# An attention, soft-MoE and feed-forward kernel: where the last back end, one expert, one copy and two steps of the background stand

## The chip, the cores and the metric

The kernel runs on one core of a Trainium2 chip. The metric is device time in microseconds (us), the median of several executions. A profiled execution gives the trace that is read here. The engines are PE (TensorE: matmuls and transposes), DVE (VectorE), ACT (ScalarE), POOL (GpSimd) and SP (SyncE, which here issues nearly all DMAs). Each runs its own instructions in order and waits on semaphores of the others.

## What is computed

Three steps, each feeding the next; B = 4, H = 8, S = 768, D = 64, 3072 tokens of 512 values, all in fp32:

```python
scores = scale * q @ k.T + bias, masked to 8 global and 96 local keys
x = softmax(scores) @ v                      # 3072 x 512

logits = x @ phi                             # 32 slots, 4 for each of 8 experts
d = softmax(logits, over tokens);  slot_input = d.T @ x
slot_out[e] = relu(slot_input[e] @ w1[e]) @ w2[e]
y = softmax(logits, over slots) @ slot_out   # 3072 x 512, of rank 32

h = y @ w_in                                 # 512 -> 2048
out = (relu(h) ** 2) @ w_out                 # 2048 -> 512
```

The feed-forward input y is a product of a 3072 x 32 matrix of weights (here c_tok, spread out as cst) with slot_out, so the kernel never forms y: for each part of w_in it computes U = slot_out @ w_in (32 rows) and then h from U.

## The kernel before

**Attention.** 48 units are worked in pairs; a unit is a pair of heads of a chunk of 256 tokens, and four units make a chunk. A unit goes through stage_qk (scores), stage_max, stage_exp, stage_T (transposes), stage_ev (copies out of PSUM, pT), stage_pv (value products, o) and stage_x (ACT copies o into the chunk's tile xT). The order on every engine is the order in which the program is written; there is no scheduler.

**Routing.** For each chunk of 256 tokens the generator `route(k)` makes the logits (into c_tok) and adds the chunk to the running softmax over tokens. Its front end makes the logits and the scaled rows xb; its back end, done for two chunks at a time, makes transposed logits pq, their maximum rmax, nm, the exponent dT (ACT, with the correction factor fo), the transposes pd of it, their copy db, the denominators rden, the product pS and its addition to acc. The generator stops at each `yield`; `step(n)` resumes the one at the head of a queue n times, `next(last)` resumes the last chunk's own (`tail`), so attention and routing are woven together by hand. In the tail the logits are made in two halves: `products(pl, range(2))` needs the first two units of the chunk, `products(pl, range(2, 4))` all four; `scaled` and `added` (DVE: lh, l, c_tok) weight and sum them, `turn` (PE: px) transposes xT. From the last chunk's pq the chain goes on through rmax, nm, dT, pd, db, pS, acc and pv to slotZ, the slots' input.

**Experts.** `w1_of(e)` multiplies slotZ by w1 of one expert on PE. The first EARLY experts come ahead of a branch (`tc.If`, into a general path that these inputs don't take), the others behind it. The weights lie in slots of SBUF: w2_0 to w2_2 are loaded when attention's tiles are given up, w2_3, w2_4, w2_5, w2_6, win_0 and wout_0 (the first parts of w_in and w_out) and w2_7 (in four pieces) each when an expert's w1 has been used. All are issued by SP in that order. `w2_of(e)` then adds up pSO; the first part of w_in and w_out, whose words are 64-bit, is converted beside it (`convert`: L750 on ACT, L751, L752 and L755 on DVE; a w_out chunk ends with a cast `hi` on ACT and a subtraction `lo`). SO is pSO copied out by ACT, pst and soT its transpose.

**Feed-forward.** Five parts of w_in and w_out, of 256, 384, 512, 512 and 384 columns, each over 12 blocks of 256 tokens. `make_u` computes pu (four matmuls with soT on the part's winf), copies it out as a high and a low half (evu), adds up four row groups in a second matmul (pu2) and writes U as a high part (ACT) in all rows, with the low part in the second and the fourth group of 32 rows (DVE, L820, one subtraction for each group). `gemm1` makes h of a block, ACT and DVE its relu and square (rg), POOL the low half of that (g); `gemm2` makes acc for half a block, three matmuls to 128 columns of the part, and DVE (or ACT) adds it to oacc. Three accumulators take turns. `make_u` for the next part and the conversion of its weights are a generator (`background`), resumed some times ahead of each half block; `total` and `room` set the pace. Between w2 and the first block PE runs filler matmuls (`warm`, tile idle).

## Time and profile before

| | us |
|---|---|
| median of 3 executions | 551.76 |
| lowest, highest | 549.9, 551.92 |
| profiled execution, its own time | 549.59 |
| its span, first to last instruction | 547.6 |
| PE busy in the span | 526.8 (96%) |
| DVE busy | 398.1 (73%) |
| ACT busy | 310.7 (57%) |
| POOL busy | 164.2 (30%) |

Attention takes the time until about 190 us, its tail and the first w1 matmul until 201, the experts until 238, the hand-over to the feed-forward until 244; the five parts then begin at about 245, 286, 345, 418 and 491 us. The share of PE is that of a busy engine, not of one at its peak. A row of a timeline gives the start, the duration, the engine, the line, the operation, what it writes and reads, the shape and a count; in brackets stands how long the engine had been idle before it and which operation released it. PEld is PE's weight load.

### The profile page before, as it was taken

Reading aid. Unit: us, or ns where it says so; the run is one execution under the profiler, and the core shown is the slowest. Engines: PE = TensorE matmul, PEld = TensorE weight load, DVE = VectorE, ACT = ScalarE, POOL = GpSimd, SP = SyncE. Lnnn points to the kernel's source line nnn. Section 1 sums busy time; section 2 is a strip of 40 time slices with the busy share of each in tenths; the row PEclk is TensorE's granted clock in tenths of the full one; section 3 lists DMA queues with packets and bytes.
Section 4 is the critical chain, followed back from the end, with each engine's and each line's share of the span. In section 5 each row is a group of like instructions: output and inputs, shape, how many; then the busy total and the mean of one; then the engine's idle time right before and its main releaser. Section 6 shows DMA issues by size and latency. Waiting matters only on the chain.

```text
span 547.6 us, 10220 instructions
## 1 busy us (share of the span) xinstructions
PE 526.8 (96%) x3669; PEld 396.9 (72%) x3669; DVE 398.1 (73%) x999; ACT 310.7 (57%) x815; POOL 164.2 (30%) x146
## 2 busy tenths in 40 slices
PE   6999999999999899989999999999999999999997
PEld 4677677777777744346878678878888878888885
DVE  4988979888888773549769797888856866645553
ACT  2888777778787611246676465545544545434441
POOL 0000000000000001014565367454754436534441
PEclk9899999999999999999999999999999999999999
DMA  7579998898972589962240404030020000003333
GB/s 258 194 252 314 314 322 304 313 338 304 317 248 85 203 312 426 414 279 58 97 154 1 154 0 156 0 116 0 21 96 1 0 2 0 1 0 116 116 116 115
DMA packets 25831, 89.20 MB, mean 163 GB/s; under 512 B 3120, under 2 KB 3760, under 8 KB 23600
## 3 DMA queue, kind: packets, MB, share of 16 engines
q1 hardware_dynamic: 25344, 88.37, 44.5%
q8 instruction: 30, 0.49, 0.4%
q14 instruction: 25, 0.20, 0.1%
q10 hardware_dynamic: 432, 0.13, 0.1%
HBM read 82.20 MB, written 6.29 MB: 162 GB/s over the span
## 4 chain that ended last, share of the span: by engine, by line
PE 44%; DVE 12%; DMA 3%; ACT 2%; issue 1%; POOL 0%; DVEq 0%; ACTq 0%; POOLq 0%
PE acc L860 13%; PE acc L861 13%; PE acc L862 13%; PE h L842 3%; DMA raw<-in_w_in 3%; DVE rg L847 2%; DVE cvyo L752 2%; DVE cvyi L752 1%; DVE cvyi L751 1%; DVE oacc L868 1%; ACT rg L846 1%; DVE cvyo L755 1%; DVE cvyo L751 1%; PE pu L801 1%; DVE winf L755 1%
## 5 line engine op out<-in xcount | busy, mean ns | idle before, releaser
L850 POOL TENSOR_TENSOR g<-rg,g 128x512 fp32r<-128x512 f32 (+1 forms) x109 | 136.2, 1251 | 174.5 <-DVE rg L847 169.2
L860 PE MATMUL acc<-w,g 128*128 128x512 f32 x384 | 151.6, 395 | 1.1 <-ACT g L849 0.6
L861 PE MATMUL acc<-w,g 128*128 128x512 f32 x384 | 150.7, 392 | 0.0
L862 PE MATMUL acc<-w,g 128*128 128x512 f32 x384 | 150.1, 391 | 0.6 <-POOL g L850 0.5
L846 ACT ACTIVATE rg<-h 128x512 f32<-128x512 f32 (+1 forms) x109 | 59.7, 547 | 118.6 <-PE h L842 114.2
L868 DVE TENSOR_TENSOR oacc<-acc,oacc 128x512 f32<-128x512 f32 x95 | 65.3, 688 | 60.8 <-PE acc L862 60.6
L255 ACT ACTIVATE sm<-sm,nm 128x256 f32<-128x256 f32 (+1 forms) x192 | 92.7, 486 | 14.3 <-DVE nm L242 11.6
L862 PEld LDWEIGHTS acc<-w,g 128*128 128x128 f32 x384 | 72.1, 188 | 18.3 <-POOL g L850 2.7
L860 PEld LDWEIGHTS acc<-w,g 128*128 128x128 f32 x384 | 72.1, 188 | 18.0 <-issue 3.2
L861 PEld LDWEIGHTS acc<-w,g 128*128 128x128 f32 x384 | 72.4, 188 | 11.2
L847 DVE SCALAR_TENSOR_TENSOR rg<-h,rg 128x512 f32<-128x512 f32 (+1 forms) x109 | 67.8, 622 | 17.2 <-ACT rg L846 17.2
L236 DVE CUSTOM_DVE_ANT_0 sm<-s,mask 128x256 f32<-128x256 f32 (+1 forms) x192 | 67.3, 396 | 1.5 <-PE s L222 1.2
L849 ACT ACTIVATE g<-rg 128x512 fp32r<-128x512 f32 (+1 forms) x109 | 63.3, 581 | 3.5
L222 PE MATMUL s<-raw 64*128 64x256 f32 (+1 forms) x384 | 52.9, 394 | 3.8 <-DVE mx L236 2.4
L388 POOL COPY l<-c_tok 128x256 f32<-128x256 f32 x11 | 4.4, 400 | 167.8 <-DVE c_tok L341 139.4
L266 PE MATMUL pt<-con,sm 128*128 128x128 f32 x352 | 47.3, 280 | 1.8 <-DVE xb L334 1.7
L283 PEld LDWEIGHTS o<-pT,v 128*64 128x64 f32 x704 | 38.0, 137 | 10.3 <-ACT pT L272 5.2
L266 PEld LDWEIGHTS pt<-con,sm 128*128 128x128 f32 x352 | 38.7, 142 | 8.9 <-DVE xb L334 3.3
L283 PE MATMUL o<-pT,v 128*64 128x128 f32 x704 | 44.3, 277 | 0.5 <-issue 0.2
L222 PEld LDWEIGHTS s<-raw 64*128 64x128 f32 x384 | 31.6, 191 | 16.2 <-issue 7.6
L842 PEld LDWEIGHTS h<-cu 128*128 128x128 f32 x192 | 35.8, 188 | 7.6 <-issue 0.3
L842 PE MATMUL h<-cu 128*128 128x256 f32 x192 | 39.8, 280 | 0.0
(150 smaller groups left out, 564.8 us busy)
## 6 DMA issues: line engine op xcount, KB each, us to landing
raw<-in_qk SPq DMA_DIRECT2D x48, 384.0 KB, 5.1
w<-in_w SPq DMA_DIRECT2D x36, 512.0 KB, 6.5
w<-in_w SPq DMA_DIRECT2D x7, 2048.0 KB, 9.5
v<-in_vx SPq DMA_DIRECT2D x48, 256.0 KB, 4.0
out_x<-oacc SPq DMA_DIRECT2D x23, 256.0 KB, 2.0
win<-in_w_in SPq DMA_DIRECT2D x2, 2048.0 KB, 7.9
wout<-in_w_out SPq DMA_DIRECT2D x2, 2048.0 KB, 8.4
win<-in_w_in SPq DMA_DIRECT2D x2, 1536.0 KB, 9.9
```

The costliest lines, as they stand in the source:

```text
L222: nc.tensor.matmul(sc[hh][:, tt, 0:n, :], lhsT=r[r0 : r0 + D, tt, :], rhs=rhs, start=True, stop=True)
L236: V.tensor_tensor_reduce(out=sm[:, j, 0:n, :], in0=sc[hh][:, tt, 0:n, :], in1=m[:, 2:3, :] if n == 1 else m[:, 0:2, :], scale=1.0, scalar= ...
L255: nc.scalar.activation(sm[:, j, 0:n, :], sm[:, j, 0:n, :], AF.Exp, bias=nm[:, j : j + 1], scale=QK_SCALE, accum_out=chunk_sums(i // NPR)[: ...
L266: nc.tensor.transpose(pp[tt][:, hh, c, :], sm[:, 2 * tt + hh, c, :], ident)
L283: nc.tensor.matmul(o[hh * D : hh * D + D, tt, :], lhsT=v[:, tt + 2 * c, hh * D : hh * D + D], rhs=pT[:, 2 * tt + hh, c, :], start=c == 0, ...
L842: nc.tensor.matmul(ph[:, k, :], lhsT=U[:, c0 : c0 + P], rhs=cst[:, n * TB : n * TB + TB], start=True, stop=True)
L847: V.scalar_tensor_tensor(g, ph[:, k0:k1, :], 0.0, r, op0=ALU.max, op1=ALU.mult)
L850: G.tensor_tensor(g2[:, 1, js, :], g, g2[:, 0, js, :].bitcast(F32), op=ALU.subtract)
L860: nc.tensor.matmul(pa, lhsT=ghi[:, j, ms], rhs=whi[:, j, :], start=j == 0, stop=False)
L861: nc.tensor.matmul(pa, lhsT=ghi[:, j, ms], rhs=wlo[:, j, :], start=False, stop=False)
L862: nc.tensor.matmul(pa, lhsT=glo[:, j, ms], rhs=whi[:, j, :], start=False, stop=j == J - 1)
L868: V.tensor_tensor(o, pa, o, op=ALU.add)
```

## The change

Four edits, the last with a change of pace:

- The back end of the last pair of chunks (9 and 10) is resumed in more and smaller pieces between the steps of the last chunk. The last chunk's generator gets one more `yield` behind the second half of its products; its first products stand directly behind the last stage_pv, ahead of pd; db and rden of the pair stand behind the first half of the logits on DVE; pS stands behind px on PE.
- EARLY is 6: the sixth expert's w1 stands ahead of the branch, and with it the issue of w2_6's load.
- The last w_out chunk of the first part is converted up to its second `yield` as before, but its cast and subtraction come behind SO and soT.
- The low part of U is one operation over all 128 rows: `U * odd + pu2`, where odd is -1 in the two groups and 0 elsewhere, a column written by three memsets on POOL.
- `background` has three `yield`s in place of one between the conversion of w_in and make_u, and `total` is larger by two.

```diff
             products(pl, range(2, 4))
+            yield
             scaled(l5[:, :, 1:5, :], 4, 8)
@@ tail of attention
     stage_pv(i)
     stage_x(i)
-    step(1)
     stage_pv(i + 1)
-    step(2)
     last = route(NU // NPR - 1, True)
     next(last)
     step(1)
     stage_x(i + 1)
+    step(2)
     next(last)
     step(1)
     next(last)
-    step(1000)
+    next(last)
+    step(2)
     queue.append(last)
@@ experts
-    EARLY = 5
+    EARLY = 6
@@ behind the branch
+    odd = ex.tile([P, 1], F32, tag="odd", name="odd")
+    G.memset(odd, 0.0)
+    for r0 in (NS, 3 * NS):
+        G.memset(odd[r0 : r0 + NS], -1.0)
@@ make_u
         nc.scalar.copy(U, pu2[:, 0:W])
-        for r0 in (NS, 3 * NS):
-            V.tensor_tensor(U[r0 : r0 + NS, :], pu2[r0 : r0 + NS, 0:W], U[r0 : r0 + NS, :].bitcast(F32), op=ALU.subtract)
+        V.scalar_tensor_tensor(U, U.bitcast(F32), odd, pu2[:, 0:W], op0=ALU.mult, op1=ALU.add)
@@ w2 of expert 6
-            for c in conv_out(0):
-                for _ in c:
-                    pass
+            c0, c1 = conv_out(0)
+            for _ in c0:
+                pass
+            next(c1)
+            next(c1)
@@ behind soT
+    for _ in c1:
+        pass
@@ background
-        for _ in range(1):
+        for _ in range(3):
             yield
@@ pace
-            total, room = 5 * (WIDTHS[q + 1] // P) + 5, 2 * (NBLK - AHEAD) - 1
+            total, room = 5 * (WIDTHS[q + 1] // P) + 7, 2 * (NBLK - AHEAD) - 1
```

PE in the tail of attention, before; o is the value product, pl and pl_2 are the two halves of the last logits:

```order
L283 MATMUL o_2932<-pT_2902,v_2776 64x128 x8
L434 MATMUL pd_2941<-con,dT_2927 128x32 x4
L326 MATMUL pl_2948<-phib,xT_2852 128x64 x4
L326 MATMUL pl_2_2965<-phib,xT_2852 128x64 x4
L452 MATMUL pS_2972<-xb_2632,db_2955 32x512 x2
L452 MATMUL pS_2972<-xb_2802,db_2955 32x512 x2
L331 MATMUL px_0_2949<-con,xT_2852 128x128 x4
```

The same place after:

```order
L283 MATMUL o_2923<-pT_2902,v_2776 64x128 x8
L326 MATMUL pl_2934<-phib,xT_2852 128x64 x4
L435 MATMUL pd_2951<-con,dT_2945 128x32 x4
L326 MATMUL pl_2_2962<-phib,xT_2852 128x64 x4
L331 MATMUL px_0_2935<-con,xT_2852 128x128 x4
L453 MATMUL pS_2976<-xb_2632,db_2967 32x512 x2
L453 MATMUL pS_2976<-xb_2802,db_2967 32x512 x2
```

The first half of the logits has moved ahead of pd, and px ahead of pS. DVE at the same place, before:

```order
L439 COPY db_2955<-pd_2941 128x128
L440 SCALAR_TENSOR_TENSOR rden<-rden,fo_2925,dn_2926 128x1
L366 TENSOR_SCALAR rc_2946<-sums_2700 128x16
L367 RECIPROCAL rc_2946<-rc_2946 128x16
L338 TENSOR_TENSOR lh_2961<-pl_2948,rc_2946 128x2x128
L341 TENSOR_REDUCE l_2962<-lh_2961 128x2x32
L338 TENSOR_TENSOR l_2962<-pl_2_2965,rc_2946 128x2x128
```

And after:

```order
L366 TENSOR_SCALAR rc_2932<-sums_2700 128x16
L367 RECIPROCAL rc_2932<-rc_2932 128x16
L338 TENSOR_TENSOR lh_2958<-pl_2934,rc_2932 128x2x128
L341 TENSOR_REDUCE l_2959<-lh_2958 128x2x32
L440 COPY db_2967<-pd_2951 128x128
L441 SCALAR_TENSOR_TENSOR rden<-rden,fo_2943,dn_2944 128x1
L338 TENSOR_TENSOR l_2959<-pl_2_2962,rc_2932 128x2x128
```

db and rden have moved from the front to between the two halves. ACT between w2 and the feed-forward, before:

```order
L790 CAST w_10268<-cvyo_10270 128x512
L750 ACTIVATE cvxo_10277<-raw_10117 128x512
L790 CAST w_10268<-cvyo_10278 128x512
L904 COPY SO<-pSO 128x512
L808 COPY evu_10324<-pu_10319 128x256
```

And after:

```order
L795 CAST w_10281<-cvyo_10283 128x512
L755 ACTIVATE cvxo_10290<-raw_10130 128x512
L911 COPY SO<-pSO 128x512
L795 CAST w_10281<-cvyo_10291 128x512
L813 COPY evu_10337<-pu_10332 128x256
```

SO and the second cast have changed places. DVE in the second part, while the third part's w_in is converted, from the third chunk's last operation on, before:

```order
L755 SCALAR_TENSOR_TENSOR winf_10746<-cvxi_10815,cvyi_10816 128x512
L868 TENSOR_TENSOR oacc_10349<-acc_2_0_10839,oacc_10349 128x512
L847 SCALAR_TENSOR_TENSOR rg_4_0_10853<-h_4_0_10850,rg_4_0_10853 128x512
L751 TENSOR_SCALAR cvyi_10859<-win_10742 128x512
L752 SCALAR_TENSOR_TENSOR cvyi_10859<-win_10742,cvyi_10859 128x512
L868 TENSOR_TENSOR oacc_10349<-acc_2_1_10863,oacc_10349 128x512
L847 SCALAR_TENSOR_TENSOR rg_4_1_10876<-h_4_1_10874,rg_4_1_10876 128x256
L755 SCALAR_TENSOR_TENSOR winf_10746<-cvxi_10858,cvyi_10859 128x512
L868 TENSOR_TENSOR oacc_10349<-acc_3_0_10882,oacc_10349 128x512
L847 SCALAR_TENSOR_TENSOR rg_5_0_10896<-h_5_0_10893,rg_5_0_10896 128x512
L805 TENSOR_TENSOR evu_10906<-pu_10901,evu_10906 128x512
L868 TENSOR_TENSOR oacc_10349<-acc_3_1_10909,oacc_10349 128x512
```

And after:

```order
L760 SCALAR_TENSOR_TENSOR winf_10757<-cvxi_10826,cvyi_10827 128x512
L756 TENSOR_SCALAR cvyi_10851<-win_10753 128x512
L757 SCALAR_TENSOR_TENSOR cvyi_10851<-win_10753,cvyi_10851 128x512
L873 TENSOR_TENSOR oacc_10361<-acc_2_0_10855,oacc_10361 128x512
L852 SCALAR_TENSOR_TENSOR rg_4_0_10869<-h_4_0_10866,rg_4_0_10869 128x512
L760 SCALAR_TENSOR_TENSOR winf_10757<-cvxi_10850,cvyi_10851 128x512
L873 TENSOR_TENSOR oacc_10361<-acc_2_1_10875,oacc_10361 128x512
L852 SCALAR_TENSOR_TENSOR rg_4_1_10888<-h_4_1_10886,rg_4_1_10888 128x256
L873 TENSOR_TENSOR oacc_10361<-acc_3_0_10893,oacc_10361 128x512
L852 SCALAR_TENSOR_TENSOR rg_5_0_10907<-h_5_0_10904,rg_5_0_10907 128x512
L873 TENSOR_TENSOR oacc_10361<-acc_3_1_10912,oacc_10361 128x512
L852 SCALAR_TENSOR_TENSOR rg_5_1_10925<-h_5_1_10923,rg_5_1_10925 128x256
```

The last winf has moved ahead of the addition of acc_2_1, and evu behind that of acc_3_1. On PE, pu stands behind acc_3_1 instead of ahead of it, in all four parts that have one; pu2 keeps its place in the second and third part and moves by one half block in the first and fourth.

## Rows read from the trace of the kernel before

**Rows 1.** Stretches: us; PE, PEld, DVE, ACT, POOL busy; PEclk, DMA share, GB/s.

```profile
11.00:18.00 7.00, 5.39 (x28) 3.76 (x30) 6.83 (x35) 4.75 (x20) 1.51 (x5) 0.51 0.67 237
18.00:176.00 158.00, 154.56 (x1644) 114.28 (x1640) 133.33 (x545) 127.30 (x459) 3.60 (x9) 1.00 0.81 280
...
201.00:205.00 4.00, 4.00 (x44) 1.27 (x40) 2.89 (x6) 0.84 (x1) 0.00 (x0) 1.00 0.52 137
205.00:236.00 31.00, 30.04 (x256) 10.87 (x246) 14.90 (x28) 7.14 (x14) 1.83 (x1) 1.00 1.01 422
```

**Rows 2.** Timeline: SP's issue of w2_3, and PE at the last quarter of w2_7.

```profile
202.50 0.33 SPq L203 DMA_DIRECT2D w<-in_w  x1
...
235.99 1.05 PE L741 MATMUL pSO<-w,hZ 128*32 128x512 f32 x4 [0.22 <-DMA w<-in_w]
```

**Rows 3.** Timeline of the tail of attention, all engines.

```profile
189.81 0.69 ACT L424 ACTIVATE dT<-pq,nm 128x512 f32<-128x512 f32 x1 [0.41 <-DVE nm L423]
...
190.64 0.43 PE L434 MATMUL pd<-con,dT 32*128 32x32 f32 x4 [0.78 <-ACT dT L424]
190.68 0.36 ACT L293 COPY xT<-o 128x256 f32<-128x256 f32 x1
...
191.00 2.00 PE L326 MATMUL pl<-phib,xT 128*128 128x64 f32 x16
191.11 0.29 DVE L439 COPY db<-pd 128x128 f32<-128x128 f32 x1 [1.33 <-PE pd L434]
...
192.14 0.42 DVE L338 TENSOR_TENSOR lh<-pl,rc 128x256 f32<-128x256 f32 x1 [0.24 <-PE pl L326]
...
193.19 0.41 DVE L338 TENSOR_TENSOR l<-pl,rc 128x256 f32<-128x256 f32 x1
...
194.27 0.74 DVE L469 SCALAR_TENSOR_TENSOR acc<-acc,fo,pS 128x512 f32<-128x512 f32 x1
...
194.51 0.65 PE L406 MATMUL pq<-con,c_tok 128*32 128x128 f32 x16
...
195.22 0.42 DVE L422 TENSOR_REDUCE rmax<-pq 128x1 f32<-128x256 f32 x1 [0.21 <-PE pq L406]
```

**Rows 4.** Timeline of the hand-over from w2 to the feed-forward.

```profile
237.20 0.62 ACT L790 CAST w<-cvyo 128x512 fp32r<-128x512 f32 x1 [2.03 <-DVE cvyo L755]
237.73 0.58 ACT L904 COPY SO<-pSO 128x512 f32<-128x512 f32 x1
...
238.36 1.08 PE L909 MATMUL pst<-con,SO 128*128 128x32 f32 x8 [0.45 <-ACT SO L904]
...
241.54 1.58 PE L79 MATMUL idle<-con 128*128 128x256 bf16 x13
...
242.14 0.86 DVE L820 TENSOR_TENSOR cu<-pu,cu 32x256 fp32r<-32x256 f32 x2 [2.37 <-ACT cu L818]
```

**Rows 5.** PE's timeline at pu in the first, second and third part.

```profile
256.95 0.84 PE L801 MATMUL pu<-winf,soT 128*32 128x384 f32 x4
...
259.15 0.50 PE L860 MATMUL acc<-w,g 128*128 128x512 f32 x1
...
302.00 1.06 PE L801 MATMUL pu<-winf,soT 128*32 128x512 f32 x6
...
304.80 0.50 PE L860 MATMUL acc<-w,g 128*128 128x512 f32 x1
...
306.97 0.28 PE L842 MATMUL h<-cu 128*128 128x256 f32 x1
...
365.74 1.06 PE L801 MATMUL pu<-winf,soT 128*32 128x512 f32 x8
```

**Rows 6.** PE's timeline late in the second part.

```profile
326.28 0.47 PE L860 MATMUL acc<-w,g 128*128 128x512 f32 x1 [0.63 <-ACT g L849]
```

**Rows 7.** DVE's groups by shape: count, busy us, mean ns, idle before them.

```profile
L752 DVE SCALAR_TENSOR_TENSOR cvyi<-win,cvyi 128x512 int32<-128x512 int32 x14 | 18.3, 1308 | 0.5
...
L752 DVE SCALAR_TENSOR_TENSOR cvyi<-raw,cvyi 128x512 int32<-128x512 int32 x2 | 1.4, 692 | 0.1
```

## Prediction

> **What bounds the kernel now.** Read the stretches first [rows 1]: the columns to look at are PEclk, the DMA share and GB/s. TensorE's granted clock is at the upper level, 2.4 GHz (1.00), in every stretch from 18 us on, of which three stand there, and at 0.51 in one before. The DMA engines are full, share 1.01 at 422 GB/s, from 205 to 236 us, and half empty (137 GB/s) in the 4 us ahead of it. So the end of the w2 stage is a matter of when that transfer train sets off, and of nothing that PE does in between. Its first car is the load of w2_3, which SP issues at 202.50, when the matmuls of the first expert's w1 have freed the slot; its last is the last quarter of w2_7, for which PE waits at 235.99 [rows 2]. What comes ahead of 202.50, the tail of attention, therefore moves the start of the feed-forward part one for one, as long as the DMA engines still have an idle stretch to give up.
>
> Then the tail, in order of time [rows 3]. The exponent dT of the last chunk pair ends at 190.50. PE has finished its value products by 189.86 (the row of pd says 0.78 us idle before 190.64, ended by dT) and stands still, though the first half of the last chunk's logit products needs nothing but xT, which is there. Those 2.00 us of pl start at 191.00 behind pd; VectorE does lh at 192.14, l at 193.19; behind l comes c_tok, and pq follows at 194.51. The chain runs on from pq to slotZ and w1.
>
> Then the hand-over [rows 4]. The last pSO matmuls end at 235.99 + 1.05 = 237.04, but ScalarE copies SO at 237.73, behind a cast that ran from 237.20. Then come pst at 238.36 and the chain to U, whose two subtractions take 0.86 together.
>
> Then the feed-forward parts. From PE's own rows [rows 5] the four matmuls of pu (the next part's U) take 1.06 us when all of winf is there (365.74). In the first part they and their wait fill 256.95 to 259.15, 2.20 us, in the second 302.00 to 304.80, 2.80 us: PE stands in its queue for VectorE's last conversion, with gemm2 matmuls behind that could run. One late wait more is the row at 326.28 [rows 6]. From 345 us on PE has no such row.
>
> **The change, part by part.** Every size is made against the profiled execution, 549.59 us with a span of 547.58.
>
> *Spread back end.* The first half of pl (2.00 / 2 = 1.00 us) goes into PE's idle stretch from 189.86 and ends near 190.85; pd follows at about its old time, since dT ends at 190.50 anyway; the second half can start near 191.1, when xT's last copy ends at 190.68 + 0.36. VectorE's lh was ready 1.14 us after pl's start (192.14 less 191.00) and so comes near 191.0, 1.15 earlier. From lh to l is 1.05 as before. But db (0.29) and the short rden now stand between them, where lh's wait used to hide them: some 0.3 lost, an estimate from the row of db. So l, c_tok and pq come 0.85 to 0.95 earlier. Behind c_tok, acc (0.74) used to fit into the wait for pq (194.27 to 195.01, rmax at 195.22); pS now starts behind px and ends about when acc wants it, so it still just fits. I take 0.9; the ends are 0.3 (pS late, acc pushes rmax) and 1.2 (nothing lost to db). The step is carried by the train: slotZ, w1_0, the issue at 202.50 and the last landing move together. The idle DMA stretch before it is 4 us, so it can give up 0.9.
>
> *Six experts ahead of the branch.* The same matmuls, and the same branch, one expert later. On SP the load of w2_6 moves ahead of the branch, and the loads of win_0, wout_0 and w2_7 queue behind the branch instead. With a full train [rows 1] an issue that comes a few us earlier or later changes no landing. On GpSimd three small memsets follow the branch, long before U reads them. I cost it at nothing. If the train had run dry the branch would show; an issue would have to slip by many us for that.
>
> *SO ahead of the cast.* SO starts when pSO ends, near 237.1 in place of 237.73: 0.6 off the path; ends 0.3 and 0.65. The cast (0.62) and the subtraction behind it move behind SO and soT, into time in which ScalarE and VectorE wait for PE; their result is first read by gemm2, behind U and gemm1.
>
> *U in one operation.* Two operations over 32 partitions take 0.86; one over 128 partitions with the same 256 elements has no row of before, but time goes by elements, so 0.42 to 0.47. The gain of about 0.4 meets PE's 13 filler matmuls, which run from 241.54 for 1.58 us until 243.12 whatever U does. PE gets at most the queue's slack back: I take 0.15, ends 0 and 0.43. In the later parts it takes 0.5 to 0.7 from VectorE, in the next step's account.
>
> *Two more steps ahead of make_u.* pu moves behind one more half block of gemm2. In the first part VectorE's conversions keep their order; pu without a wait costs 0.8 at three quarters of the columns of the row at 365.74, and I allow 0.3 for the half block, which may have to wait for its accumulator: 2.20 - 0.8 - 0.3 = 1.1, ends 0.3 and 1.4. In the second part the quicker pace also puts the last winf ahead of two VectorE operations, and pu wants it a half block later (304.80 to 306.97, 2.17 us): 2.80 less 1.06 = 1.74, I take 1.7, ends 0.8 and 1.75. The gap from pu to pu2 shrinks to one such half block there; a cast and a subtraction lie between, some 1.4 us by the cast at 237.20 (0.62) and acc (0.74). The conversions of w_out start one step later and are still done before the next part. In the fourth and third part nothing waits now, nothing to gain.
>
> *Late waits.* The PE wait at 326.28 (0.63 us), and about as much again spread over both parts, come from VectorE working behind. The change moves conversions behind accumulator additions there and takes a U operation out: I take 0.8, ends -0.5 (conversions now late) and 2.0.
>
> **Sum:** 0.9 + 0.6 + 0.15 + 1.1 + 1.7 + 0.8 = 5.25 us. On the profiled execution that is 549.59 to 544.3; on the median of the runs shown, 551.76, it is 546.5. Two of the three runs lie 2.2 us above the profiled one, one 0.3 above; the forecast is for the median, and this spread is in the range.
>
> **A rule weighed.** VectorE's L752 (two SBUF inputs) took 692 ns in the tail, where GpSimd is silent, and 1308 ns on average in the parts, where GpSimd subtracts [rows 7]. The Trainium skill (SBUF — State Buffer, Who interferes with whom) says that VectorE and GpSimd share a port pair as an exclusive lock, and that an operation with two SBUF inputs is blocked for the whole of a GpSimd operation that reads SBUF. By that rule the trace agrees, and moved conversions land behind other GpSimd subtractions: if each of the moved ones were blocked, the feed-forward gain would mostly go, and the sum would be that of the first rival; by the rows alone it stays at 5.25.
>
> **Rivals.** (1) *VectorE stays the bound.* The two steps only move the wait: conversions stretched from 0.69 to 1.31 or more arrive as late as PE's new place for pu, or accumulators are freed late. For it: the row of L752, and the accumulator wait that I already count in the first part. Against it: pu's new place is up to 2.17 us later. Then only the tail and the hand-over remain, 1.65 us: 550.1. (2) *VectorE catches up wholly.* The late waits vanish, and the upper ends hold: about 6.9 us, 544.9. (3) *The train does not move*, since its first car only waits for the load before it: 5.25 - 0.9 gives 547.4. Against it: the half empty stretch [rows 1]. (4) *Slower: the clock falls.* In the stretch 11 to 18 us the granted clock is 0.51, 1.2 GHz, after PE had been only partly busy; each such 7 us costs up to 3.5 us of matmul time. Place: the hand-over, where PE lives on fillers whose spacing moves. Two such stretches cost 7 and turn 546.5 into 553.5; it decides from 1.5 stretches. Against it: the change takes idle time out, and the rows show 1.00 in all that time. The Trainium skill (TensorE: Matmul & The Clock Gate, What's actually happening) says that the throttled state is the default and activity releases it; by that rule too, less idle time speaks against a fall.
>
> **How the numbers follow.** Forecast 0.52, rival 1 0.20, rival 2 0.15, rival 3 0.08, rival 4 0.03, other 0.02. A measurement of this kernel can tell about 0.5% from no change, 2.76 us, so 549.0 divides. Faster: forecast, rivals 2 and 3 and a little of rival 1, 0.76; same: the rest of rival 1 and other, 0.21; slower 0.03. The range takes in rival 2 from the lower run (549.9 less 6.5, 543.4) and ends at 549.7, where half of rival 1 and rival 4 are left out.
>
> **What would show it.** Right: pq about 4.7 us after the end of the value products is down by 0.9, the w2_3 issue is near 201.6; SO starts within 0.1 of pSO's end; the pu rows of the first two parts have no wait and take 0.8 and 1.06; the second part shrinks by 1.7 or more. Wrong: pu still waiting for winf, or pu2 for evu; an accumulator wait ahead of the half block in front of pu; a granted clock under 1.00 after 18 us; the last w2_7 quarter still landing near 235.9.

## The result and the profile after

| | before | after |
|---|---|---|
| median, us (runs beside each other) | 551.83 (4) | 545.76 (4) |
| lowest, highest | 549.9, 551.92 | 545.5, 546.05 |
| profiled execution, its own time | 549.59 | 546.05 |
| its span | 547.6 | 544.0 |

The ratio is 0.9907, 95% interval 0.9887 to 0.9927: faster by 0.9%. The medians lie 6.07 us apart, the two profiled executions 3.54. The forecast of 546.5 for the median was right within 0.8 us. Much of what follows is about why these two differences, 6.07 and 3.54, are not the same: a pair of traces explains the second only.

The stretches of [rows 1], after (us; PE, PEld, DVE, ACT, POOL busy; PEclk, DMA share, GB/s):

```profile
11.00:18.00 7.00, 5.23 (x24) 3.60 (x26) 6.83 (x35) 4.58 (x18) 1.53 (x5) 0.59 0.68 241
...
201.00:205.00 4.00, 4.00 (x44) 1.23 (x40) 2.93 (x5) 0.84 (x1) 0.00 (x0) 1.00 0.67 215
205.00:236.00 31.00, 29.79 (x249) 10.48 (x241) 14.31 (x28) 7.16 (x14) 2.54 (x4) 1.00 1.01 420
```

The train of weights set off earlier (215 GB/s in the stretch from 201 us, 137 before) and is full from 205 us on, as before. SP's issue of w2_3 and PE's last quarter of w2_7, the two rows of [rows 2]:

```profile
202.03 0.33 SPq L203 DMA_DIRECT2D w<-in_w  x1
...
236.00 1.05 PE L746 MATMUL pSO<-w,hZ 128*32 128x512 f32 x4 [0.22 <-DMA w<-in_w]
```

The issue is 0.47 us earlier, the last quarter is not (236.00 against 235.99). The tail, all engines, against [rows 3]:

```profile
190.07 1.10 PE L326 MATMUL pl<-phib,xT 128*128 128x64 f32 x8
190.09 0.69 ACT L425 ACTIVATE dT<-pq,nm 128x512 f32<-128x512 f32 x1 [0.42 <-DVE nm L424]
...
191.11 0.43 PE L435 MATMUL pd<-con,dT 32*128 32x32 f32 x4
191.21 0.42 DVE L338 TENSOR_TENSOR lh<-pl,rc 128x256 f32<-128x256 f32 x1 [0.78 <-PE pl L326]
191.47 1.10 PE L326 MATMUL pl<-phib,xT 128*128 128x64 f32 x8
...
193.85 0.65 PE L407 MATMUL pq<-con,c_tok 128*32 128x128 f32 x16
194.10 0.75 DVE L470 SCALAR_TENSOR_TENSOR acc<-acc,fo,pS 128x512 f32<-128x512 f32 x1 [0.31 <-PE pS L453]
...
194.77 0.42 DVE L423 TENSOR_REDUCE rmax<-pq 128x1 f32<-128x256 f32 x1
```

Everything ahead of the tail ends 0.28 us later in this execution (dT at 190.09 against 189.81), in code that the change leaves as it was. Measured from dT, pq comes at 3.76 us instead of 4.70: 0.94 earlier. The pd row has no idle time in brackets any more. But acc waits 0.31 us for pS and then holds up rmax, which starts only 0.73 earlier, from dT (4.68 against 5.41).

The hand-over, against [rows 4]:

```profile
237.10 0.58 ACT L911 COPY SO<-pSO 128x512 f32<-128x512 f32 x1 [1.78 <-PE pSO L746]
237.58 0.62 ACT L795 CAST w<-cvyo 128x512 fp32r<-128x512 f32 x1
237.76 1.06 PE L916 MATMUL pst<-con,SO 128*128 128x32 f32 x8
...
240.91 1.58 PE L79 MATMUL idle<-con 128*128 128x256 bf16 x13
...
241.57 0.48 DVE L825 SCALAR_TENSOR_TENSOR cu<-cu,odd,pu 128x256 fp32r<-128x256 f32 x1 [1.83 <-ACT cu L823]
242.25 0.72 PE L847 MATMUL h<-cu 128*128 128x256 f32 x4
```

SO starts 0.05 after pSO's end (236.00 + 1.05), the cast runs behind it beside PE's pst, and U's low part is one operation of 0.48 us.

And pu in the first and the second part, against [rows 5], on PE's timeline:

```profile
257.85 0.85 PE L806 MATMUL pu<-winf,soT 128*32 128x384 f32 x8
...
303.17 1.06 PE L806 MATMUL pu<-winf,soT 128*32 128x512 f32 x8
```

All eight matmuls stand in one row, with no wait: 0.85 and 1.06 us. What PE waits for in the two parts altogether is a view of its own: waits of PE from the part's first gemm2 matmul to the next part's (engine, line, releaser: us in total, times, longest). First part before:

```profile
PE pu L801 <- DVE winf L755: 0.6, 1, 0.6
PE acc L862 <- POOL g L850: 0.5, 2, 0.3
PE acc L860 <- DVE oacc L866: 0.4, 2, 0.3
```

First part after:

```profile
PE acc L865 <- DVE oacc L871: 1.0, 4, 0.4
PE acc L867 <- POOL g L855: 0.7, 3, 0.2
```

Second part before; after, the same view has no row at all:

```profile
PE pu L801 <- DVE winf L755: 0.8, 1, 0.8
PE acc L860 <- ACT g L849: 0.6, 1, 0.6
```

In the second part the waits are gone. In the first the wait of pu has been replaced by waits for accumulators.

**Where the 3.6 us of the span lie**, by the starts of rows: the tail begins 0.28 later; dT to the issue of w2_3 11.94 us instead of 12.69 (-0.75); from there to the last quarter of w2_7 33.97 instead of 33.49 (+0.48); from there to the first gemm2 7.65 instead of 8.55 (-0.90); first part 41.50 instead of 41.63 (-0.13); second 56.00 instead of 58.61 (-2.61); the other three within 0.01. Together 3.63, against 3.58 by the spans (547.58 and 543.96).

### The profile page after: what moved, and what is told of

Read it like the earlier page. It is cut to its first block, busy times and chain, and to the rows that moved or that the text cites. A ratio compares the mean times of both kernels' runs of the same rounds, so it can differ in the third digit from the quotient of the medians.

```text
span 544.0 us, 10228 instructions
## 1 busy us (share of the span) xinstructions
PE 526.0 (97%) x3669; PEld 397.2 (73%) x3669; DVE 396.8 (73%) x994; ACT 310.4 (57%) x815; POOL 164.3 (30%) x149
## 4 chain that ended last, share of the span: by engine, by line
PE 48%; DVE 7%; DMA 4%; ACT 1%; issue 1%; POOL 1%; SPq 0%; DVEq 0%; POOLq 0%
PE acc L865 14%; PE acc L866 14%; PE acc L867 14%; DMA w<-in_w 4%; PE h L847 3%; DVE rg L852 1%; DVE cvyi L757 1%; DVE cvyi L756 1%; DVE cvyo L757 1%; PE pre L654 1%; DVE oacc L871 1%; PE pu L806 1%; DVE winf L760 1%; DVE oacc L873 1%; PE idle L79 1%
## 5 line engine op out<-in xcount | busy, mean ns | idle before, releaser
L222 PEld LDWEIGHTS s<-raw 64*128 64x128 f32 x384 | 31.6, 191 | 15.7 <-issue 7.6
```

The costliest lines, as they stand in the source:

```text
L222: nc.tensor.matmul(sc[hh][:, tt, 0:n, :], lhsT=r[r0 : r0 + D, tt, :], rhs=rhs, start=True, stop=True)
```

## Experiments

Twelve runs followed, eleven with an edit of their own and after_again, which is the changed kernel once more. The table gives for the profiled execution of each, in us: A, start of the last eight value products to the issue of w2_3; B, first to last w1 matmul; C, issue of w2_3 to the last quarter of w2_7; D, from there to the first gemm2 matmul; and the first two parts, from the first gemm2 matmul of each to that of the next. All are differences of starts on PE's and SP's timelines. The third and fourth part took 73.20 and 72.61 in all of them, the fifth, up to the start of its last gemm2 matmul, 52.76 (within 0.02).

| kernel | experts ahead | A | B | C | D | part 1 | part 2 |
|---|---|---|---|---|---|---|---|
| before | 5 | 13.28 | 13.74 | 33.49 | 8.55 | 41.63 | 58.61 |
| tail_alone | 5 | 12.54 | 13.74 | 33.59 | 8.50 | 41.62 | 58.62 |
| hand_alone | 5 | 14.86* | 13.74 | 33.58 | 7.65 | 41.40 | 58.01 |
| pace_alone | 5 | 13.27 | 13.73 | 33.54 | 8.54 | 42.32 | 56.37 |
| early_alone | 6 | 13.28 | 14.49 | 33.51 | 10.50* | 41.66 | 58.63 |
| fill_alone | 5 | 13.27 | 13.73 | 33.87 | 8.74 | 41.68 | 58.62 |
| after | 6 | 12.53 | 14.31 | 33.97 | 7.65 | 41.50 | 56.00 |
| after_again | 6 | 12.53 | 14.52 | 33.69 | 7.65 | 41.51 | 56.01 |
| after_early5 | 5 | 12.53 | 13.74 | 33.53 | 7.65 | 41.49 | 56.01 |
| after_lo_dve | 6 | 12.53 | 14.48 | 33.65 | 7.65 | 41.94 | 55.99 |
| after_lo_later | 6 | 12.52 | 14.72 | 34.43 | 7.65 | 42.42 | 56.02 |
| after_fill | 6 | 12.62 | 16.12 | 33.40 | 8.40 | 41.56 | 56.03 |
| after_idle | 6 | 12.53 | 14.59 | 34.59 | 9.32* | 41.56 | 56.03 |
| candidate | 5 | 12.61 | 13.72 | 33.42 | 7.73 | 42.41 | 55.99 |

A star marks a stretch in which the granted clock fell (below). The times, each with runs of the kernel before beside it:

| kernel | median, us (runs) | lowest to highest | median of before | ratio, 95% interval |
|---|---|---|---|---|
| tail_alone | 549.76 (12) | 548.68 to 551.24 | 551.49 (35) | 0.9979 (0.9966 to 0.9992) |
| hand_alone | 549.01 (12) | 547.21 to 550.46 | 551.49 | 0.9956 (0.9941 to 0.9971) |
| pace_alone | 549.64 (12) | 548.24 to 550.41 | 551.49 | 0.9972 (0.996 to 0.9984) |
| early_alone | 551.68 (12) | 550.31 to 552.37 | 551.49 | 1.001 (0.9998 to 1.0022) |
| after_again | 545.78 (5) | 545.53 to 547.19 | 550.34 (15) | 0.992 (0.9899 to 0.9942) |
| fill_alone | 550.15 (11) | 549.83 to 550.47 | 550.34 | 0.9987 (0.9975 to 0.9999) |
| after_early5 | 545.9 (5) | 545.18 to 546.87 | 550.34 | 0.9923 (0.9901 to 0.9945) |
| after_lo_dve | 546.01 (5) | 545.82 to 548.71 | 550.34 | 0.9933 (0.9906 to 0.9959) |
| after_lo_later | 546.65 (6) | 546.37 to 547.59 | 551.45 (11) | 0.9923 (0.9907 to 0.9938) |
| after_fill | 546.49 (6) | 545.73 to 547.49 | 551.45 | 0.9921 (0.9904 to 0.9938) |
| after_idle | 546.34 (6) | 545.33 to 548.4 | 551.45 | 0.9916 (0.9895 to 0.9936) |
| candidate | 546.78 (6) | 546.45 to 548.13 | 551.45 | 0.9927 (0.9911 to 0.9944) |

### One part at a time

**The tail alone.**

```diff
-    step(1)
     stage_pv(i + 1)
-    step(2)
     last = route(NU // NPR - 1, True)
     next(last)
     step(1)
     stage_x(i + 1)
+    step(2)
     next(last)
     step(1)
     next(last)
-    step(1000)
+    next(last)
+    step(2)
```

> The kernel before with the spread back end alone; experts, hand-over and pace as they were. Theory A (the prediction's: the transfer train moves with the tail): pq starts 0.9 us earlier than in the kernel before, so do slotZ, the issue of w2_3 and the last landing of w2_7, and the time falls by 0.9 us. Theory B (from the changed kernel's trace: w2_3 was issued 0.47 us earlier and PE still got the last quarter of w2_7 at 236.00, where it had been 235.99): slotZ comes 0.5 to 0.7 us earlier measured from the last value products, the last quarter of w2_7 starts on PE at the old time, and the time falls by 0 to 0.2 us.

Measured: A is 0.74 shorter, and C is 33.59, so here the train does move with its first car; the last quarter of w2_7:

```profile
235.55 1.05 PE L742 MATMUL pSO<-w,hZ 128*32 128x512 f32 x4 [0.22 <-DMA w<-in_w]
```

That speaks for theory A and against what the changed kernel's own trace seemed to say. The second witness is the trace of hand_alone, where the tail lasted 1.58 longer (14.86) for a reason of its own: its last quarter came at 237.97, 1.98 later than before's, with C unchanged at 33.58. The median fell by 1.73 us, more than twice the 0.74 of the path. Neither theory has an account of that; the set on the clock has a part of it.

**SO and U alone.**

```diff
-            for c in conv_out(0):
-                for _ in c:
-                    pass
+            c0, c1 = conv_out(0)
+            for _ in c0:
+                pass
+            next(c1)
+            next(c1)
@@ behind soT
+    for _ in c1:
+        pass
@@ make_u
-        for r0 in (NS, 3 * NS):
-            V.tensor_tensor(U[r0 : r0 + NS, :], ...)
+        V.scalar_tensor_tensor(U, U.bitcast(F32), odd, pu2[:, 0:W], op0=ALU.mult, op1=ALU.add)
```

> The kernel before with SO ahead of the cast and U's low parts in one operation; tail, experts and pace as they were. Theory A (the prediction's terms): 0.6 us from SO and 0.15 from U at the hand-over, the parts unchanged: 0.75 us less. Theory B (from the changed kernel's trace, where the first gemm1 came 0.90 us earlier against the last quarter of w2_7): 0.9 us less at the hand-over, and in the first four parts a U operation that is 0.3 to 0.5 us shorter on VectorE shortens no wait of PE: 0.9 in all. If VectorE being behind is what makes the late waits, the second part gets shorter too, by up to 1.1 us: 2.0 in all.

Measured: D 0.90 shorter, first part 0.23 shorter, second 0.60: 1.73 in all by the trace, theory B with a good part of its last sentence. SO and U were not run apart: of the 0.90, 0.62 lie between the last quarter and pst, the rest behind it. The median fell by 2.48. The twelve runs form two groups, six at 547.21 to 548.36 and six at 549.66 to 550.46; the profiled one (549.87) is of the upper.

**The pace alone.**

```diff
-        for _ in range(1):
+        for _ in range(3):
@@
-            total, room = 5 * (WIDTHS[q + 1] // P) + 5, 2 * (NBLK - AHEAD) - 1
+            total, room = 5 * (WIDTHS[q + 1] // P) + 7, 2 * (NBLK - AHEAD) - 1
```

> The kernel before with the three yields and the larger total alone; tail, experts, SO and U as they were. Theory A (the prediction's terms): first part 1.1 us less, second 1.7 less, late waits 0.8 less, 3.6 us in all. Theory B (from the changed kernel's trace): the wait at pu goes in both parts, 1.1 and 1.9 us; in the first part 1.0 comes back as new waits in blocks 4, 7 and 8, because the conversions of w_out move behind GpSimd's subtractions; in the second the late waits go: 0.1 + 2.6 = 2.7 us in all. If the U operation and not the pace takes the late waits of the second part away, they are still here (1.1 us) and only 1.6 us are gained.

Measured: second part 2.24 shorter, first part 0.69 longer, 1.55 in all by the trace, close to the last sentence of theory B, though by another sum; 1.85 by the medians. PE's waits in the first part of this kernel:

```profile
PE acc L860 <- DVE oacc L866: 1.7, 4, 1.1
PE acc L862 <- POOL g L850: 0.7, 3, 0.2
```

One accumulator alone is waited for 1.1 us. So in the first part the two edits belong together: the pace takes the wait of pu away and makes VectorE late for the accumulators; the shorter U operation takes most of that back (41.50 with both).

**Six experts alone.**

```diff
-    EARLY = 5
+    EARLY = 6
```

> The kernel before with six experts ahead of the branch in place of five, nothing else. Theory A (the prediction's): no difference, 0 us, because the train of weights is full and ends at the same time. Theory B (from the changed kernel's trace, where the w1 matmuls of the last experts ended 0.57 us later against their start, with PE idle in two places behind the branch): the w1 stage gets 0.5 us longer, the last quarter of w2_7 still starts on PE at the old time, 0 us. Theory C: the loads that stand behind w1 on SP land later, and the time rises by 0.5 us.

Measured: B is 0.75 longer, C is as before (33.51), the median 0.19 higher with 1.0 inside the interval. Theory B, as far as this run tells. The long D of 10.50 is not theirs; it leads to the next set.

### The granted clock

The profiled executions of hand_alone and early_alone are both long in one place. Here are the windows of the first in the tail (columns as in [rows 1]):

```profile
190.00:192.00 2.00, 1.22 (x14) 1.02 (x11) 0.63 (x5) 1.22 (x4) 0.00 (x0) 1.00 0.85 205
...
193.00:194.00 1.00, 1.00 (x11) 0.32 (x10) 0.97 (x3) 0.00 (x0) 0.00 (x0) 0.71 1.00 426
194.00:195.00 1.00, 1.00 (x9) 0.03 (x1) 0.66 (x1) 0.00 (x0) 0.00 (x0) 0.50 1.11 475
195.00:196.00 1.00, 1.00 (x8) 0.69 (x4) 0.75 (x1) 0.00 (x0) 0.00 (x0) 0.50 0.81 344
```

and of early_alone in the hand-over, with the thirteen fillers that [rows 4] has at 1.58 us:

```profile
238.00:240.00 2.00, 1.02 (x9) 0.97 (x8) 0.69 (x1) 0.98 (x2) 0.00 (x0) 1.00 1.00 424
240.00:241.00 1.00, 0.62 (x9) 0.16 (x8) 0.29 (x1) 0.00 (x0) 0.00 (x0) 1.00 1.07 455
...
242.00:243.00 1.00, 1.00 (x5) 0.52 (x4) 0.00 (x0) 0.25 (x1) 0.00 (x0) 0.50 0.15 61
243.00:244.00 1.00, 1.00 (x6) 0.70 (x5) 0.83 (x2) 0.12 (x1) 0.00 (x0) 0.50 0.00 0
244.00:245.00 1.00, 1.00 (x6) 0.75 (x5) 0.02 (x1) 0.00 (x0) 0.00 (x0) 0.50 0.00 0
```

```profile
242.51 2.95 PE L79 MATMUL idle<-con 128*128 128x256 bf16 x13
```

In both, PE stood still for a part of the time (busy 1.22 of 2 us, 1.64 of 3), and a little later the granted clock is at 0.50, 1.2 GHz, for some 3 us; the fillers take 2.95 us in place of 1.58, and A is 1.58, D 1.95 us longer. The code of early_alone is that of before in both places, of hand_alone in the tail. The Trainium skill (TensorE: Matmul & The Clock Gate, What's actually happening) says that the throttled state is the default and that activity releases it; these rows agree. They add that such a stretch is not always followed by a fall: before's own trace has 1.36 of 2 us busy at 190 to 192, 1.25 of 2 at 238 to 240, and 1.00 after both.

So a new theory: before's runs, 65 in all beside the various kernels, are a mixture. 30 lie below 551.1 us (26 of them at 549.74 to 550.48, median of the 30 550.16), 35 above (551.17 to 552.42, median 551.78), and the upper ones are those in which the clock fell in one of the two places. The profiled execution, 549.59, is of the lower kind, and no upper run of before itself was traced. But the record lists the mean granted clock of 61 of the 65 runs. Of the 32 upper ones 27 have 0.992 or less (mean 0.990), of the 29 lower ones 24 have 0.993 or more (mean 0.994). Some 3 us at half speed take about 1.5 / 548 = 0.003 off that mean (an estimate from the rows above), so the two groups differ by about one fall. One run alone can't be told by this figure: early_alone's profiled execution has the fall and 0.993, before's has none and 0.993. Four kernels were run on it.

**The changed kernel again.** No edit.

> The changed kernel itself, more executions. In the four runs done by now it lay between 545.5 and 546.05 us, while 35 runs of the kernel before fell into two groups (549.85 to 550.99 and 551.17 to 552.42). Theory C (clock): the upper group of before holds executions in which TensorE's granted clock is at half for some 3 us, in the tail of attention (as in the trace of the run of the hand-over alone, 0.50 at 194 to 196 us) or in the hand-over (as in that of the six experts alone, 0.50 at 242 to 245 us), each time behind a stretch in which PE stood idle; the changed kernel has less idle time in both places, so nearly all of its runs lie in one group, between 545.3 and 546.5. Theory D (chance): the four runs happened to miss it, and about half of the runs now lie some 1.5 us higher.

Measured: four runs at 545.53 to 545.95 and one at 547.19. With the first four that makes eight of nine in one group, where before has under half, and all nine have a mean clock of 0.993 or more. That is theory C, but for the one run at 547.19: its clock is 0.993, so it may be high for another reason.

**Only fillers.** Nothing of the change; 16 more filler matmuls where PE stands idle:

```diff
     stage_pv(i + 1)
+    gap = aps.tile([P, 512], F32, tag="s", name="gap", bufs=4)
+    warm(6, con, gap)
     step(2)
@@ hand-over
-    warm(7, con, idle)
+    warm(12, con, idle)
@@ behind pst
+    warm(3, con, idle)
@@ ahead of the first h
-    warm(13, con, idle)
+    warm(15, con, idle)
```

> The kernel before with nothing of the change, but with more filler matmuls on PE: six between the last value products and pd, five more behind w2, three between pst and pu, two more ahead of the first h. They stand where PE waits for another engine and should delay nothing. Theory C (clock): idle time on PE is what lets the granted clock fall; with it filled the upper group of the kernel before (12 to 20 of 35 runs at 551.2 to 552.4) goes, all runs lie at 549.8 to 550.7, and the median falls by 1 to 1.5 us, to about 550.2. Theory D (chance, or a cause outside PE): both groups stay, the median stays within 0.3 us of before's.

Measured: all eleven runs lie at 549.83 to 550.47, where six of the fifteen of before beside them lie above 551.1. The upper group is gone, and the lower one is where it was. The mean clock is 0.993 or more in all eleven. In the profiled execution D is 0.19 longer and no stretch is shorter by more than 0.01, so all that the fillers gain is that the upper runs are gone. The median did not fall by over 1 us as expected, since this time before's own median was of its lower group (550.34). The distribution is theory C's.

**Idle time put back.** The changed kernel without two groups of fillers:

```diff
     nc.scalar.copy(SO, pSO)
     idle = bps.tile([P, 512], F32, tag="post", name="idle4", bufs=2)
-    warm(7, con, idle)
@@
-    warm(5, con, idle)
     next(u, None)
```

> The changed kernel with two of its groups of fillers in the hand-over left out (the seven ahead of pst and the five ahead of the second pu), so that PE stands idle where it did not. The fillers are no part of the result, so on the undisturbed path the time is that of the changed kernel, 545.7, or up to 0.1 less. Theory C (clock): PE's idle time lets the granted clock fall, the rows of the next few us stand at 0.50, and half of the runs or more lie 1 to 2.5 us higher, the median near 547. Theory D: the distribution is that of the changed kernel, the median 545.7.

Measured: three runs at 545.33 to 545.77, three at 546.91 to 548.4. The profiled one, 548.4, has the fall in the hand-over:

```profile
238.00:240.00 2.00, 1.22 (x12) 1.11 (x16) 0.49 (x2) 0.86 (x2) 0.00 (x0) 1.00 1.00 424
240.00:241.00 1.00, 0.49 (x8) 0.01 (x2) 0.40 (x1) 0.37 (x1) 0.00 (x0) 1.00 0.93 393
...
242.00:243.00 1.00, 1.00 (x7) 0.69 (x6) 0.41 (x1) 0.37 (x1) 0.00 (x0) 0.50 0.06 25
```

```profile
241.89 2.93 PE L79 MATMUL idle<-con 128*128 128x256 bf16 x13
```

Of the three upper runs the two highest, 548.21 and 548.4, have a mean clock of 0.987 and 0.989, 546.91 has 0.994: two falls of six rather than the half that theory C expected, and the median rose by 0.6 only. In the profiled run the fall makes D 1.67 longer; another 0.6 lies in C (34.59 against 33.97), at a granted clock of 1.00. Idle time taken out removes the upper runs (none of 11, against 6 of 15), idle time put in brings falls (two of 6, one of them traced, where the changed kernel's nine have no clock below 0.993). The numbers are small, but both point the same way.

The clocks of the one-part runs fit this too. hand_alone leaves the tail as it was: the six runs of its upper group have 0.991 each, the lower six 0.992 to 0.997. pace_alone leaves both places as they were: six of twelve have 0.991. tail_alone has 0.992 or less in three of twelve only. So tail_alone's median also falls because fewer of its runs have a fall; how much of its 1.73 that is was not worked out.

**Fillers on top of the change.**

```diff
-                warm(3, con, idle)
+                warm(8, con, idle)
@@ behind pv
+            if banks[0] is aps:
+                warm(4, con, idle)
@@ behind pst
+    warm(3, con, idle)
```

> The changed kernel with more filler matmuls where PE still stands idle in the tail and the hand-over: five more ahead of the last pd, four behind pv, three between pst and pu. Theory C (clock): the few executions that lie 1 to 3 us higher (547.19 of five, 548.71 and 546.87 in two neighbours of five) are executions in which the granted clock fell; with less idle time all runs lie at 545.3 to 546.1, the median at 545.7. Theory D: the high ones stay as frequent, about one in five; the median stays within 0.3 us.

Measured: 545.73 to 547.49, no tidy group, and a median 0.7 above the changed kernel's. Theory C fails here: what is left of high runs of the changed kernel is not cured by fillers. Nor are they falls of the clock, as far as the record tells: all six runs have 0.993 to 0.997, the two highest 0.994 and 0.997. What makes them high stays open. One candidate is the train: the profiled run of after_lo_later lies at 547.5, 0.9 above that kernel's median, with C at 34.43 and a granted clock of 1.00 there. This trace shows another loss, which belongs to the next set.

### Six experts ahead of the branch, once more

**Five again, in the changed kernel.**

```diff
-    EARLY = 6
+    EARLY = 5
```

> The changed kernel with five experts ahead of the branch, as before the change. The tail alone moved the last quarter of w2_7 0.44 us earlier (235.55), in the changed kernel it did not move (236.00). Theory A: the sixth expert ahead of the branch is what holds the train back in the changed kernel, through the later issue of win_0's neighbours and w2_7 (215.01 against 214.35 with the tail alone); undone, the last quarter comes near 235.6 and the time falls by 0.4 to 0.5 us, to 545.3. Theory B: the sixth expert costs nothing, and the landing differs by chance of the transfers; the time is the same within 0.2 us.

Measured: C is 33.53 and the last quarter comes at 235.17, but this execution began 0.39 earlier too; the two lowest runs, 545.18 and 545.2, are the lowest of all, the two highest are 546.87. In time it can't be told from the changed kernel. In the table it can: B is 13.72 to 13.74 in all seven executions with five experts ahead, and 14.31 to 16.12 in all seven with six. C is 33.42 to 33.59 with five (33.87 once), and with six anything from 33.40 to 34.59. The cause of the longer B is in PE's timeline behind the branch. Before, 48 matmuls in one piece:

```profile
209.48 5.36 PE L653 MATMUL pre<-w,slotZ 128*32 128x512 f32 x48 [0.18 <-PEq L676]
```

after_fill, where it is worst, 14 matmuls, then a gap in which PE waits for nothing that the profile shows:

```profile
210.67 1.92 PE L656 MATMUL pre<-w,slotZ 128*32 128x512 f32 x14 [0.17 <-PEq L679]
213.96 2.73 PE L656 MATMUL pre<-w,slotZ 128*32 128x512 f32 x18 [1.38 <-issue]
```

The loads of win_0, wout_0 and w2_7 stand behind these matmuls on SP; there they went out at 215.01 to 216.73 instead of 212.71 to 215.01. They landed no later for that: win_0 and wout_0 came 12.7 and 14.8 us behind their issue, at 227.7 and 230.2, in the changed kernel 15.7 and 17.8 behind it, at 228.4 and 230.9. The last quarter did not mind either (235.37). What is late is PE itself: its last pc starts at 227.78 instead of 226.03, and VectorE's operations on that pc (L725) stand ahead of the conversions, which then start without a wait for their load, at 229.94 instead of 228.41. The last conversion of wout_0 ends so late that soT has to wait for it:

```profile
228.88 1.03 DVE L725 TENSOR_TENSOR cu<-pc,cu 64x384 fp32r<-64x384 f32 x2 [1.63 <-ACT cu L724]
229.94 0.43 DVE L758 TENSOR_SCALAR cvyi<-raw 128x512 int32<-128x512 int32 x1
...
238.16 0.69 DVE L762 SCALAR_TENSOR_TENSOR cvyo<-cvxo,cvyo 128x512 int32<-128x512 int32 x1
238.89 0.29 DVE L920 COPY soT<-pst 128x128 f32<-128x128 f32 x1
```

soT could have gone at 238.45, when pst ended. ScalarE's half of the same conversion (0.68 from 236.17) had already kept SO waiting for 0.34 us. Together they are most of the 0.75 by which D is longer. The fillers are not the cause: candidate has them too, with five experts ahead, and its D is 7.73. So the sixth expert can cost something here, by the time that PE loses behind the branch, though no median shows it. What PE waits for there was not tried and stays open.

### VectorE and GpSimd in the first part

In the changed kernel's first part, VectorE's and GpSimd's timeline:

```profile
266.00 1.59 POOL L855 TENSOR_TENSOR g<-rg,g 128x512 fp32r<-128x512 f32 x1 [2.61 <-ACT oacc L871]
266.35 1.53 DVE L756 TENSOR_SCALAR cvyo<-wout 128x512 int32<-128x512 int32 x1
...
267.56 1.47 POOL L796 TENSOR_TENSOR w<-cvyo,w 128x512 fp32r<-128x512 f32 x1
267.91 1.67 DVE L757 SCALAR_TENSOR_TENSOR cvyo<-wout,cvyo 128x512 int32<-128x512 int32 x1
```

The conversions end 0.29 and 0.55 us after the GpSimd operations beside them, which end at 267.59 and 269.03. **The low part on VectorE**, three operations moved:

```diff
-            (G if q else V).tensor_tensor(lo[:, j, :], f, ...)
+            (G if q > 1 else V).tensor_tensor(lo[:, j, :], f, ...)
```

> The changed kernel, with the low part of the second part's w_out subtracted on VectorE instead of GpSimd (three operations of 128 x 512, 0.69 us each by the hand-over's row). Theory P (port): VectorE's conversions are stretched by GpSimd's operations (L756 took 1.53 us at 266.35 and L757 1.67 at 267.91, while GpSimd ran from 266.00 to 269.03, against 0.42 and 0.69 without), and that is why PE waits in blocks 7 to 9 of the first part of the changed kernel; without GpSimd's three operations the conversions get shorter by 2 to 3 us in sum, less the 2.1 us that VectorE takes over, and the first part gets 0.3 to 0.8 us shorter. Theory W (work): VectorE simply has too much to do in the first part; with 2.1 us more it gets later, and the first part grows by 0.3 to 1.0 us.

Measured: behind the moved operation the same two conversions take

```profile
267.63 0.41 DVE L756 TENSOR_SCALAR cvyo<-wout 128x512 int32<-128x512 int32 x1
268.08 0.69 DVE L757 SCALAR_TENSOR_TENSOR cvyo<-wout,cvyo 128x512 int32<-128x512 int32 x1
```

0.41 and 0.69 where GpSimd is silent. The stretching beside GpSimd is shown for single operations. The Trainium skill (SBUF — State Buffer, Who interferes with whom) has it for operations with two SBUF inputs and for those in a two-port mode; L756 has one input, so it would be of the second kind, and the trace agrees with both. But the first part grew by 0.44, to 41.94, as theory W has it: its 18 conversion operations are 2.6 us shorter in sum (14.87 against 17.47), and the three subtractions take as much again on VectorE. As VectorE stood idle 0.69 us ahead of the moved operations, **one step later** was tried:

```diff
             nc.scalar.copy(hi[:, j, :], f)
+            if q == 1:
+                yield
+            (G if q > 1 else V).tensor_tensor(lo[:, j, :], f, ...)
@@
-            total, room = 5 * (WIDTHS[q + 1] // P) + 7, ...
+            total, room = 5 * (WIDTHS[q + 1] // P) + (7 if q else 10), ...
```

> The changed kernel with the low part of the second part's w_out on VectorE and one step of the background later than in the run before (a further yield between the cast and the subtraction, total larger by three in the first part). In that run VectorE stood idle 0.69 us ahead of each of the first two subtractions, for ScalarE's cast, and the first part took 41.94 us against 41.50. Theory P (port): without GpSimd's three operations two conversions ran at 0.41 and 0.69 in place of 1.53 and 1.67; with the idle time gone as well the first part takes 40.9 to 41.3, and the time falls by 0.2 to 0.6 us against the changed kernel's undisturbed runs (545.6). Theory W (work): VectorE is the bound of the late blocks by its plain work, the first part takes 41.5 to 42.0 us.

Measured: 42.42, worse again, over theory W's own range. PE's longest wait there:

```profile
268.08 1.52 DVE L756 TENSOR_SCALAR cvyo<-wout 128x512 int32<-128x512 int32 x1
...
271.78 0.50 PE L867 MATMUL acc<-w,g 128*128 128x512 f32 x1 [0.95 <-DVE oacc L873]
```

VectorE is the bound in the late blocks (busy for 3.90 of the 4 us from 270 to 274), and what is added there comes out at an accumulator's copy. But it is not plain work alone: one step later the conversions meet GpSimd's subtractions for g instead (L756 at 268.08 again 1.52, L757 at 274.49 1.66), and their sum is back at 16.44. So the run does not part the two theories; moving one GpSimd operation away did not clear the place. The **candidate** put this together with the fillers of after_fill and five experts:

> A version meant to beat both: the changed kernel with five experts ahead of the branch, with the fillers of the second run of this set, and with the low part of the second part's w_out on VectorE one step later. By the steps: the sixth expert 0.1 us (545.2 in its two lowest runs against 545.5), the fillers nothing on the undisturbed path, the low part 0.2 to 0.6 us if the port explains the first part, so 544.9 to 545.4 and no high runs. If VectorE's plain work is the bound there, 545.5 to 546.0.

Measured: 546.45 to 546.87 in five runs of six, 0.9 us in the first part given away (42.41). Nothing that ran beats the changed kernel; with five experts it is its equal.

## Why the prediction was right, and where it was not

The number came out because two errors cancelled: 0.8 us too much on the path, and 1.6 us of which it had no account. Like for like, lower runs against lower runs, the change gives 550.16 - 545.70 = 4.46 us (545.70: median of the eight lower runs of the changed kernel), and the traces of the undisturbed path 0.74 + 0.90 + 0.13 + 2.61 = 4.4 where the train holds its length. Forecast were 5.25. The rest of the 6.07 is that the upper half of before's runs, most of them with a fall of the clock, has no counterpart after. That this made up for the 0.8 was luck.

| step | taken | shown |
|---|---|---|
| tail | 0.9 | pq 0.94, issue of w2_3 0.74 (A) |
| train carries it one for one | yes | yes (tail_alone, hand_alone); in the profiled run of the change 0.48 lost in C |
| six experts | 0 | 0 in time, within 1.2; B 0.6 to 2.4 longer |
| SO | 0.6 | 0.61 |
| U | 0.15 | 0.3 |
| pu, first part | 1.1 | 1.1 at pu, 1.0 given back |
| pu, second part | 1.7 | 1.90, less 0.44 in the next block |
| late waits | 0.8 | 1.13 in the second part, -1.0 in the first |

**Tail.** The working was right up to pq. "It still just fits" was wrong for acc: pS ended too late, acc was held 0.31 and pushed rmax. That is the mechanism of the lower end named in the prediction (0.3), but it cost 0.2 of the 0.9 and not 0.6.

**Train.** The test "the last quarter still landing near 235.9" came out against the prediction in the first trace, and rival 3 looked true. tail_alone says otherwise. One pair of traces could not settle 0.5 us there, because C alone moves by that much between executions with six experts ahead.

**Six experts.** Costed at nothing, and nothing was measured, but the reason given ("the same branch, one expert later") missed that PE stalls behind it. The reason given for the loads held: in after_fill, where they were issued 2.3 us later, win_0 and wout_0 landed no later. What came onto the path was PE's own loss behind the branch, handed on by VectorE.

**SO and U.** SO as worked out: 2.37 us from the last quarter to pst in before, 1.76 after. U gained twice what was taken: h now starts 1.34 us behind the first of the thirteen fillers (240.91 to 242.25) instead of 1.61 (241.54 to 243.15), less than the 1.58 of their row, in which the last one's end is counted. The one operation took 0.48, a little over the 0.42 to 0.47.

**pu.** Both waits went as worked out; the blocks that hold pu are 1.11 and 1.90 shorter. What the sum had wrong is where VectorE is late next. It allowed 0.3 for an accumulator in the first part; 1.0 came, in three later blocks (the fifth, the eighth, the ninth). Rival 1, VectorE stays the bound, is what happened in the first part; rival 2, it catches up wholly, in the second. The likeliest case stood between the two and was off by 0.9 (2.74 against 3.6).

**Clock.** Rival 4 had the right mechanism, one of the two places and the wrong sign. The prediction looked at the profiled execution, saw 1.00 throughout, and put the 2.2 us between before's runs down as spread to be carried along. By the clocks on record they are that mechanism at work in about half of the runs, and the change takes out idle time that sets it off. A fall costs 1.6 to 1.95 us, where the rival took up to 3.5.

**Slips that changed nothing.** The two L752 rows of 692 ns are not in the tail but beside w2 (228.73 and 230.59); GpSimd is silent there too. The range's lower bound goes by 6.5 us for rival 2, which stands at 6.9. And the edits are five, not four: U's low part is one of its own.

## What to carry to other kernels

When the runs of one kernel fall into two groups, the profiled execution shows only one of them: before a forecast for the median is made, ask which stage could hold the difference, and look there for PE idle in a program that is otherwise dense. Fillers in such a place are judged by the distribution of the times, and by the mean clock of each run, not by one trace. And where two edits touch one busy engine, each alone can say the opposite of both: the pace made the first part 0.69 longer, U made it 0.23 shorter, both together (in the changed kernel) made it 0.13 shorter.

## What was not expected of the hardware

- The granted clock falls to 0.50 for some 3 us in the middle of a program, behind a stretch in which PE was busy for 1.22 of 2 us or 1.64 of 3, in some executions and not in others: 1.6 to 1.95 us each time.
- Behind a branch that is not taken, under a full train (1.01), PE lost 0.6 to 2.4 us more in seven of seven executions, when two experts stood behind it instead of three.
- A conversion with one input in SBUF was stretched from 0.41 to 1.53 us by a GpSimd subtraction beside it, as those with two inputs were from 0.69 to 1.67.
